# A spectral-mixing and leaky-ReLU kernel: loading filter rows instead of copying them, and a new order of work in the prologue

## Chip, cores and metric

One core of a Trainium2 chip. The metric is the device time of one execution in microseconds (us). In a profile, PE is the matmul engine, DVE is VectorE, ACT is ScalarE, POOL is GpSimd.

## The reference

`x` is (8, 3008, 256), the filters are (1505, 256), `w_in` is (256, 2048), `w_out` is (2048, 256).

```python
X = np.fft.rfft(x, axis=1)
y = np.fft.irfft(X * (filt_r + 1j * filt_i)[None], n=3008, axis=1)   # 24064 tokens
h = y.reshape(24064, 256) @ w_in
out = np.maximum(0.01 * h, h) @ w_out
```

## The kernel before

The transform of a batch is four stages of matmuls with transposes between them: S1, a DVE transpose, S2 (whose result is multiplied by the filters), SA, a second transpose, SB, which writes the tokens into `yts`. The result of each matmul stage is copied out of PSUM, where matmuls write, by ACT or DVE; this is called evacuation. The program uses PSUM in banks and lets a stage write into one only after its last content has been read. From then on the two large matmuls of chunk after chunk of 512 tokens keep PE busy, and the transforms of later batches run beside them. Only the first batch's transform, the prologue, has nothing to hide behind. It is split into two halves of the channels (`hf`). DVE and Pool share the multiplication of S2's result; the filter tiles need the same rows twice, in partitions 0 to 63 and in 64 to 127.

```python
    def filt_load(dst, src, d0, dn):
        for q, first, sgn in ((0, 0, 1), (Q, N1, -1)):
            nc.gpsimd.dma_start(dst[q : q + Q, :, ds(d0, dn)], ...)   # casts to fp16
    ...
    for n0, nn in first_parts:
        x_load(0, n0, nn)                       # 4 loads
    for hf in range(2):
        filt_load(fa_sb, filt_r, hf * DH, DH)   # 2 loads each: 8 in all
        filt_load(fb_sb, filt_i, hf * DH, DH)
    nc.gpsimd.dma_start(i1_sb[:], i1_d.ap())
    nc.gpsimd.dma_start(w_in_sb[:], ...)
    ...
    def first_s2(hf, c, n, on_pool):
        ps = bank("ph", n, DH)                  # 2 banks in turn
        ...                                     # matmuls
        if on_pool:
            ...                                 # ACT copies PSUM to SBUF, Pool multiplies twice
        else:
            ...                                 # DVE multiplies twice, straight from PSUM

    def upper(hf):                              # rows 0-63 copied to 64-127
        for t, cp in ((fa_sb, act), (fb_sb, dve)):
            cp(t[64:P, :, ts(hf, DH)], t[0:64, :, ts(hf, DH)])

    def keep_warm(n):                           # matmuls on a tile of zeros
        ...
    keep_warm(28)
    ...                                         # S1 in four parts, as the parts of x land
    t1_part(0, 0, True)(), t1_part(0, 1, True)()   # the first transpose
    upper(0)
    first_s2(0, 8, 8, True)
    x_load(1)
    first_s2(0, 0, 8, False)
    t1_part(0, 2, True)()
    keep_warm(3)
    first_s2(0, 20, 4, True)                    # Pool's small block
    keep_warm(4)
    first_s2(0, 16, 4, False)
    t1_part(0, 3, True)()
    upper(1)
    first_sa(0, 0), first_sa(0, 16)
    keep_warm(3)
    first_s2(1, 8, 8, True)
    first_s2(1, 0, 8, False)                    # DVE's second half starts here
    first_sa(0, 8), first_sa(0, 20)
    keep_warm(3)
    ...                                         # w_out load
    first_s2(1, 16, 8, False)                   # DVE's last block
    keep_warm(4)
    first_sa(1, 0)
    ...                                         # other SA, second transposes
    for g in range(8):
        first_sb(g, act, ...)
    for g in range(8, 16):
        first_sb(g, (act, dve)[g % 2], ...)
```

Of the kernel before, what the change touches and what calls it, by code (L numbers as in the profile page):

```python
# [20 lines left out]
Q = 32  # L21
# [44 lines left out]
def kernel(  # L66
# [30 lines left out]
    fa_sb = cpool.tile([P, NC, D], FP16, name="fa_sb")  # L97
    fb_sb = cpool.tile([P, NC, D], FP16, name="fb_sb")
# [18 lines left out]
    def bank(kind, n, w):  # L117
        of = wide if kind == "ph" else single
        t = of[turn[kind] % len(of)]
        turn[kind] += 1  # L120
        return t[:, : n * w].rearrange("p (n w) -> p n w", n=n)
# [5 lines left out]
    DH = D // 2  # L127

    def x_load(b, n0=0, nn=N2, d0=0, dn=D):

        for lo, cnt in ((0, R1),) if b + 1 < B else ((0, 64), (64, N1 - 64)):
            nc.gpsimd.dma_start(  # L132
                x_sb[lo : lo + cnt, ds(n0, nn), ds(d0, dn)],
                bass.AP(tensor=x.tensor, offset=x.offset + (b * N + lo * N2 + n0) * D + d0,
                        ap=[[N2 * D, cnt], [D, nn], [1, dn]]))

    def filt_load(dst, src, d0, dn):

        for q, first, sgn in ((0, 0, 1), (Q, N1, -1)):
            nc.gpsimd.dma_start(  # L140
                dst[q : q + Q, :, ds(d0, dn)],
                bass.AP(tensor=src.tensor, offset=src.offset + first * D + d0,
                        ap=[[N1 * D, N2 // 2], [sgn * NC * D, 2], [sgn * D, NC], [1, dn]]))

# [8 lines left out]
    for hf in range(2):  # L153
        filt_load(fa_sb, filt_r, hf * DH, DH)
        filt_load(fb_sb, filt_i, hf * DH, DH)
    nc.gpsimd.dma_start(i1_sb[:], i1_d.ap())
    nc.gpsimd.dma_start(w_in_sb[:], moe_w_in.rearrange("(dt p) c -> p dt c", p=P))
    idle = cpool.tile([P, CH], FP16, name="idle")
# [20 lines left out]
    def paired(t):  # L179
        return t[:].rearrange("p (e n t) -> p n e t", n=Q, t=2)  # L180
# [7 lines left out]
    def t1_part(b, i, flat=False):  # L188
        def go():
            a = big[(4 * b) % 3][:].bitcast(FP32)[:, ts(i, E4 * Q)].rearrange("p (e n) -> p e n", n=Q)  # L190
            o = big[(4 * b + 1) % 3][:].bitcast(FP32)
            if flat:
                o = o[:, ts(i, E4 * Q)].rearrange("p (e n) -> p e n", n=Q)
            else:
                o = o.rearrange("p (n e) -> p e n", n=Q)[:, ts(i, E4), :]
            nc.vector.transpose(o, a)  # L196
        return go
# [49 lines left out]
    two = ("pf", "ph")  # L247
    act, dve = nc.scalar.copy, nc.vector.tensor_copy
# [9 lines left out]
    def first_s2(hf, c, n, on_pool):  # L258
        ps = bank("ph", n, DH)
        src = paired(big[1])  # L260
        for j in range(0, n, 4):
            nc.tensor.matmul(ps[:, ds(j, 4), :].rearrange("p n (e t) -> p n e t", t=2), fwd2,  # L262
                             src[:, ds(c + j, 4), ts(hf, DH // 2)], start=True, stop=True)
        fs = [f[:, ds(c, n), ts(hf, DH)] for f in (fa_sb, fb_sb)]
        if on_pool:
            y = [outp.tile([P, n, DH], FP16, tag="ost", name=f"fy{i}_h{hf}_c{c}") for i in range(2)]
            xs = [scrp.tile([P, 4, DH], FP32, tag=f"p{j // 4 + 1}", name=f"fx_h{hf}_c{c + j}")
                  for j in range(0, n, 4)]
            for j, xf in enumerate(xs):
                act(xf[:], ps[:, ts(j, 4), :])  # L270
            for i in range(2):
                for j, xf in enumerate(xs):
                    nc.gpsimd.tensor_tensor(y[i][:, ts(j, 4), :], xf[:], fs[i][:, ts(j, 4), :], AL.mult)
        else:
            y = [ypp.tile([P, n, DH], FP16, tag=f"yw{i}", bufs=2, name=f"fy{i}_h{hf}_c{c}")
                 for i in range(2)]
            for i in range(2):
                nc.vector.tensor_tensor(y[i][:], ps, fs[i], AL.mult)
        ys[(hf, c)] = y

    def first_sa(hf, c):
        y = ys.pop((hf, c))
        for j in range(0, y[0].shape[1], 4):
            ps = bank("pf", 4, DH)
            for i, m in enumerate((inv2, inv2x)):
                nc.tensor.matmul(ps, m, y[i][:, ds(j, 4), :], start=(i == 0), stop=(i == 1))  # L286
            act(paired(big[2])[:, ds(c + j, 4), ts(hf, DH // 2)],  # L287
                ps.rearrange("p n (t e) -> p n e t", t=2))


    def first_t2(i):
        a = big[2][:].bitcast(FP32)[:, ts(i, E4 * Q)].rearrange("p (e n r) -> p e n r", n=Q // 2, r=2)
        o = big[0][:].bitcast(FP32).rearrange("p (h n e r) -> p h e n r", h=2, n=Q // 2, r=2)
        nc.vector.transpose(o[:, i // 2, ts(i % 2, E4)], a)  # L294

    def first_sb(g, copy, kind):
        dt, h = g // 8, g % 8
        src = big[0][:].rearrange("p (h n e r t) -> p h n r t e", h=2, n=Q // 2, r=2, t=2)
        ps = bank(kind, 4, N1)
        for j in range(4):  # L300
            n2 = 4 * h + j
            for t in range(2):
                nc.tensor.matmul(ps[64 * t : 64 * t + 64, j, :], src[:, dt, n2 // 2, n2 % 2, t, :],  # L303
                                 i1_sb[:, n2, :], start=True, stop=True)
        yv = yts[0][:, dt, :].rearrange("p (a c) -> p a c", c=N2)
        copy(yv[:, :, ds(4 * h, 4)], ps.rearrange("p c a -> p a c"))

    def upper(hf):
        for t, cp in ((fa_sb, act), (fb_sb, dve)):
            cp(t[64:P, :, ts(hf, DH)], t[0:64, :, ts(hf, DH)])  # L310


    def keep_warm(n):
        for _ in range(n):
            nc.tensor.matmul(po_ps.rearrange("p a d -> p (a d)"), idle[:, 0:P], idle[:],  # L315
                             start=True, stop=True)

    keep_warm(28)
    g = 0
    for n0, nn in first_parts:  # L320
        while nn:
            n = 2 if nn % 4 or n0 >= N2 - 4 else 4
            first_s1(n0, n, two[n // 4], (dve, act)[g % 2])
            n0, nn, g = n0 + n, nn - n, g + 1
        keep_warm(5 if n0 < N2 else 14)
    t1_part(0, 0, True)(), t1_part(0, 1, True)()
    upper(0)
    first_s2(0, 8, 8, True)
    x_load(1)
    first_s2(0, 0, 8, False)  # L330
    t1_part(0, 2, True)()
    keep_warm(3)
    first_s2(0, 20, 4, True)
    keep_warm(4)
    first_s2(0, 16, 4, False)
    t1_part(0, 3, True)()
    upper(1)
    first_sa(0, 0), first_sa(0, 16)
    keep_warm(3)
    first_s2(1, 8, 8, True)  # L340
    first_s2(1, 0, 8, False)
    first_sa(0, 8), first_sa(0, 20)
    keep_warm(3)
    nc.gpsimd.dma_start(w_out_sb[:], moe_w_out.rearrange("(ct p) d -> p ct d", p=P))
    first_s2(1, 16, 8, False)
    keep_warm(4)
    first_sa(1, 0)
    keep_warm(4)
    first_t2(0), first_t2(1)
    first_sa(1, 16), first_sa(1, 8)  # L350
    first_t2(2), first_t2(3)
    keep_warm(3)
    for g in range(8):
        first_sb(g, act, two[(g // 2) % 2])
    for g in range(8, 16):
        first_sb(g, (act, dve)[g % 2], two[(g // 2) % 2])

    nc.gpsimd.tensor_scalar(fb_sb[64:P], fb_sb[64:P], -1.0, None, AL.mult)

# [70 lines left out]
    for slot in range(SL * (NCHUNK + 1)):  # L430
        ci, g = divmod(slot, SL)
# [36 lines left out]
```

## Time and profile before

| what | value | where from |
|---|---|---|
| median time | 784.93 us (3 runs); with three later ones 785.34 us (6 runs, 784.69 to 786.42) | timed runs |
| profiled execution | 784.44 us, span 782.6 us | profile |
| start of the first transpose | 17.03 us | DVE's timeline |
| token tile complete (last SB evacuation) | 42.75 us | DVE's timeline |
| gapless PE work begins | 53.49 us | chain that ended last |

The start of the first transpose is called **T1** here, and the way from it to the complete token tile **C**: 42.75 - 17.03 = 25.72 us. The rest, 784.44 - 42.75 = 741.69 us, is not touched by the change. The three views of this profile that the argument starts from are shown in the prediction; the end of C is the line at 42.20 of its first. Its beginning is this line of DVE's timeline (start, length, what, count):

```profile
17.03 2.37 DVE L196 STREAM_TRANSPOSE big<-big 128x1024 f32<-128x1024 f32 x2 [0.21 <-ACT big L184]
```

This is PE's timeline at the beginning (start, length, what, count):

```profile
1.20 8.34 PE L315 MATMUL po_ps<-idle 128*128 128x512 f16 x28 [1.20 <-DVE one L162]
9.38 0.38 PE L253 MATMUL pf<-x_sb,f_sb 94*128 94x256 f16 x2
```

S1 starts when the 28 warm-up matmuls end.

### The profile page before, as it was taken

To read this page: it belongs to the slowest core of one execution; us is meant where nothing else is said; L and a number is where in the kernel's file an instruction comes from. 1 tells how busy PE (TensorE), PEld (TensorE's weight loads), DVE (VectorE), ACT (ScalarE), POOL (GpSimd) and SP (SyncE) were. 2 spreads that over 40 slices of the span, in tenths; PEclk is the share of its full clock that TensorE was granted. 3 is DMA by queue.
4 is the path that set the end of the run, shared out by engine and by line. 5 is a ranking of instruction groups with operands and counts; after the bars stand their busy time and mean duration, and the time that the engine had idled before them with its cause. 6 is when DMAs were issued, how large, how long until landed. Compare 5 with 4: busy or idle time off the path is not lost.

```text
span 782.6 us, 13696 instructions
## 1 busy us (share of the span) xinstructions
PE 775.5 (99%) x5853; PEld 532.1 (68%) x5853; DVE 366.4 (47%) x458; ACT 556.1 (71%) x790; POOL 148.9 (19%) x122
## 2 busy tenths in 40 slices
PE   9999999999999999999999999999999999999998
PEld 4356677666776677766777667776677666676666
DVE  4868751875237641477306754088432765200000
ACT  4786759776686767777687775967768776666664
POOL 4864300250004300052001510025000340000000
PEclk9999999999999999999999999999999999999999
DMA  9952102301041101510105101140101001101111
GB/s 186 216 83 59 41 28 54 97 28 41 28 103 46 41 28 41 107 42 29 41 28 114 35 29 40 42 106 28 41 28 40 30 28 41 41 28 40 42 41 54
DMA packets 36252, 43.38 MB, mean 55 GB/s; under 512 B 8130, under 2 KB 34370, under 8 KB 35522
## 3 DMA queue, kind: packets, MB, share of 16 engines
q0 software_dynamic: 10000, 16.99, 12.4%
q1 hardware_dynamic: 26192, 25.53, 9.3%
q8 instruction: 45, 0.74, 0.4%
q14 instruction: 15, 0.12, 0.1%
HBM read 34.10 MB, written 24.64 MB: 75 GB/s over the span
## 4 chain that ended last, share of the span: by engine, by line
PE 93%; ACT 2%; DVE 1%; issue 1%; ACTq 0%
PE po_ps L390 41%; PE ph L376 41%; PE pf L173 3%; PE pf L240 2%; PE pf L213 2%; PE pf L228 2%; PE pf L390 1%; ACT big L184 1%; ACT gt_c L381 1%; PE ph L262 0%; PE pf L286 0%; DVE big L294 0%; PE po_ps L315 0%; ACT big L287 0%; PE ph L303 0%
## 5 line engine op out<-in xcount | busy, mean ns | idle before, releaser
L381 ACT ACTIVATE gt_c<-ph 128x1024 f16<-128x1024 f32 x376 | 384.8, 1024 | 194.8 <-PE ph L376 193.2
L376 PE MATMUL ph<-yt,w_in_sb 128*128 128x512 f16 (+7 forms) x1728 | 386.7, 351 | 0.4 <-ACT gt_c L381 0.2
L390 PE MATMUL po_ps<-w_out_sb,gt_c 128*128 128x256 f16 x2944 | 381.5, 272 | 0.5 <-ACT ost_c_t L397 0.5
L390 PEld LDWEIGHTS <-gt_c 128*128 128x128 f16 x3008 | 290.6, 98 | 86.8 <-issue 1.7
L376 PEld LDWEIGHTS <-w_in_sb 128*128 128x128 f16 x1728 | 162.9, 98 | 95.3 <-issue 1.0
L221 POOL TENSOR_TENSOR y_b_g<-p_b_g,p_b_g 128x512 f16<-128x512 f32 x84 | 106.9, 1273 | 225.5 <-DVE p_b_g L219 225.5
L196 DVE STREAM_TRANSPOSE big<-big 128x1024 f32<-128x1024 f32 x32 | 55.9, 1844 | 127.1 <-ACT big L184 127.0
L184 ACT CAST big<-pf 128x512 f16<-128x512 f32 x190 | 109.0, 607 | 1.1 <-PE pf L253 1.1
L243 DVE CAST yt<-pf 128x376 f16<-128x376 f32 x112 | 56.3, 544 | 85.7 <-PE pf L240 85.7
L217 DVE TENSOR_TENSOR p_b_g<-pf,fa_sb 128x512 f32<-128x512 f32 x84 | 58.1, 692 | 38.5 <-PE pf L213 35.9
L397 ACT COPY ost_c_t<-po_ps 128x256 f32<-128x256 f32 x184 | 69.4, 377 | 6.7 <-PE po_ps L390 5.6
L204 DVE STREAM_TRANSPOSE big<-big 128x1024 f32<-128x1024 f32 x28 | 51.1, 1934 | 34.7 <-ACT big L184 34.7
L218 DVE TENSOR_TENSOR p_b_g<-pf,fb_sb 64x512 f32<-64x512 f32 x84 | 58.2, 692 | 1.1
L219 DVE TENSOR_TENSOR p_b_g<-pf,fb_sb 64x512 f32<-64x512 f32 x84 | 57.4, 683 | 1.1
L132 POOL DMA_DIRECT2D x_sb<-in_x_dram x12 | 6.6, 553 | 255.4 <-PE pf L173 254.6
L240 PEld LDWEIGHTS <-big 128*128 128x128 f16 x448 | 25.6, 98 | 13.2
L173 PE MATMUL pf<-x_sb,f_sb 94*128 94x256 f16 x224 | 33.8, 272 | 0.1
L213 PE MATMUL pf<-big,small_sb 128*128 128x512 f16 x84 | 31.8, 379 | 0.0
L228 PE MATMUL pf<-y_b_g,small_sb 128*128 128x512 f16 x84 | 31.8, 379 | 0.0
L240 PE MATMUL pf<-i_sb,big 128*128 128x94 f16 x448 | 28.7, 206 | 0.0
L173 PEld LDWEIGHTS <-f_sb 94*128 94x128 f16 x224 | 21.0, 97 | 9.5 <-issue 1.3
L315 PE MATMUL po_ps<-idle 128*128 128x512 f16 x81 | 21.6, 411 | 1.2 <-DVE one L162 1.2
(46 smaller groups left out, 158.4 us busy)
## 6 DMA issues: line engine op xcount, KB each, us to landing
out_dram<-ost_c_t SPq DMA_DIRECT2D x92, 256.0 KB, 2.1
x_sb<-in_x_dram POOLq DMA_DIRECT2D x6, 1536.0 KB, 11.2
x_sb<-in_x_dram POOLq DMA_DIRECT2D x3, 480.0 KB, 9.3
w_in_sb<-in_moe_w_in_dram POOLq DMA_DIRECT2D x1, 1024.0 KB, 14.1
w_out_sb<-in_moe_w_out_dram POOLq DMA_DIRECT2D x1, 1024.0 KB, 11.0
x_sb<-in_x_dram POOLq DMA_DIRECT2D x1, 1024.0 KB, 8.0
f_sb<-fwd_const SPq DMA_DIRECT2D x4, 192.0 KB, 4.8
fa_sb<-in_filt_r_dram POOLq DMA_DIRECT2D x4, 192.0 KB, 12.1
```

Source lines behind the costliest of these rows:

```text
L173: nc.tensor.matmul(ps[:, j, :], f1_sb[:N1, n2, :], x_sb[:N1, n2, :], start=True, stop=True)
L184: copy(paired(dst)[:, ds(n0, nn), ds(e0, de)], ps.rearrange("p n (e t) -> p n e t", t=2))
L217: nc.vector.tensor_tensor(p1[:], ps, fa, AL.mult)
L218: nc.vector.tensor_tensor(p2[0:64], ps[64:P], fb[64:P], AL.mult)
L219: nc.vector.tensor_tensor(p2[64:P], ps[0:64], fb[0:64], AL.mult)
L221: nc.gpsimd.tensor_tensor(y1[:], p1[:], p2[:], AL.add)
L240: nc.tensor.matmul(ps[:, j, :], src[:, dt, n2, :], i1_sb[:, n2, :], start=True, stop=True)
L243: copy(yv[:, :, ds(4 * h, 4)], ps.rearrange("p c a -> p a c"))
L376: nc.tensor.matmul(ph[:, j, ds(o, ln)], w_in_sb[:, dt, ts(ct, P)], yts[b % 2][:, dt, ds(lo, ln)], start=(dt == 0), stop=(dt == NDT - 1),)
L381: nc.scalar.activation(gts[ci][:, ds(2 * g, 2), :], ph, AF.Lrelu)
L390: nc.tensor.matmul(po, gts[ci][:, ct, ts(tj, P)], w_out_sb[:, ct, :], start=(ct == 0), stop=(ct == NCT - 1))
L397: nc.scalar.copy(ost[:, tj % 2, :], po)
```

## The change

The intent: take the second half's two copies off ACT and DVE by loading the upper rows from memory; give DVE its S2 first; let DVE take group 8 of the last evacuations as well; drop nine warm-up matmuls that are then not needed.

```diff
-    def filt_load(dst, src, d0, dn):
+    def filt_load(dst, src, d0, dn, up=0):
...
+    filt_load(fa_sb, filt_r, DH, DH, 64)
+    filt_load(fb_sb, filt_i, DH, DH, 64)
     nc.gpsimd.dma_start(i1_sb[:], i1_d.ap())
...
     upper(0)
+    first_s2(0, 0, 8, False)
     first_s2(0, 8, 8, True)
     x_load(1)
-    first_s2(0, 0, 8, False)
     t1_part(0, 2, True)()
-    keep_warm(3)
-    first_s2(0, 20, 4, True)
     keep_warm(4)
     first_s2(0, 16, 4, False)
+    first_s2(0, 20, 4, True)
     t1_part(0, 3, True)()
-    upper(1)
     first_sa(0, 0), first_sa(0, 16)
     keep_warm(3)
+    first_s2(1, 0, 8, False)
     first_s2(1, 8, 8, True)
-    first_s2(1, 0, 8, False)
     first_sa(0, 8), first_sa(0, 20)
-    keep_warm(3)
+    keep_warm(2)
...
     first_s2(1, 16, 8, False)
-    keep_warm(4)
     first_sa(1, 0)
...
-    keep_warm(3)
+    keep_warm(2)
...
-        first_sb(g, (act, dve)[g % 2], two[(g // 2) % 2])
+        first_sb(g, act if g in (10, 12, 14) else dve, two[(g // 2) % 2])
```

More of the change, by code (lines that the diff above doesn't have):

```diff
@@ L135, in x_load @@
                         ap=[[N2 * D, cnt], [D, nn], [1, dn]]))
-    def filt_load(dst, src, d0, dn):
+    def filt_load(dst, src, d0, dn, up=0):
         for q, first, sgn in ((0, 0, 1), (Q, N1, -1)):
             nc.gpsimd.dma_start(
-                dst[q : q + Q, :, ds(d0, dn)],
+                dst[up + q : up + q + Q, :, ds(d0, dn)],
                 bass.AP(tensor=src.tensor, offset=src.offset + first * D + d0,
```

## The prediction

> **What bounds the kernel now.** I read the page's busy shares first: PE 775.5 us of a 782.6 us span. The change touches only the prologue, the first 43 us in which the FFT of the first batch is made and no output matmul can run yet. PE's 99% says nothing there, since 81 of its matmuls are warm-up ones on a tile of zeros (21.6 us). So the useful view is the chain that ended last, cut to the first 75 us:
>
> ```profile
> 25.51 0.60 DVE fy_h_c L278
> 26.11 1.16 DVE big L196
> ...
> 35.07 2.18 ACT big L287 x4
> ...
> 37.27 2.38 DVE big L294 x2
> ...
> 42.20 0.56 DVE yt L306
> ...
> 53.49 1.97 PE ph L376 x8
> ```
>
> The reader should see three stretches. Up to about 42.8 us VectorE, ScalarE and short matmuls hand over to each other. From 43.6 to 53.5 us the chain is ScalarE's (each 1.02 us activation plus evacuations of batch 1's first stage). After 53.49 us it is PE without a gap to the end. Hence whatever shortens or lengthens the way to 42.8 us moves the end by the same amount, and nothing else in the change can: at most a few us of 785.
>
> The second view is VectorE's timeline in the prologue:
>
> ```profile
> 19.44 0.95 DVE L310 COPY fb_sb<-fb_sb 64x3072 f16<-64x3072 f16 x1
> 21.43 1.23 DVE L278 TENSOR_TENSOR fy_h_c<-ph,fa_sb 128x1024 f16<-128x1024 f32 x1 [1.04 <-ACT fx_h_c L270]
> ...
> 26.04 1.22 DVE L196 STREAM_TRANSPOSE big<-big 128x1024 f32<-128x1024 f32 x1
> 27.29 2.07 DVE L310 COPY fb_sb<-fb_sb 64x3072 f16<-64x3072 f16 x1
> 29.39 1.22 DVE L278 TENSOR_TENSOR fy_h_c<-ph,fa_sb 128x1024 f16<-128x1024 f32 x1
> 30.53 1.21 DVE L278 TENSOR_TENSOR fy_h_c<-ph,fb_sb 128x1024 f16<-128x1024 f32 x1
> 32.12 1.22 DVE L278 TENSOR_TENSOR fy_h_c<-ph,fa_sb 128x1024 f16<-128x1024 f32 x1 [0.37 <-PE ph L262]
> 33.26 1.21 DVE L278 TENSOR_TENSOR fy_h_c<-ph,fb_sb 128x1024 f16<-128x1024 f32 x1
> ```
>
> Two things are to be seen: an idle 1.04 us before the first product (PE first made the S2 for Pool, then the one for DVE), and a copy of 2.07 us that holds the second half. The third view is Pool's timeline:
>
> ```profile
> 15.76 0.58 POOL L156 DMA_DIRECT2D i_sb<-inv_const  x1
> 16.73 0.72 POOL L157 DMA_DIRECT2D w_in_sb<-in_moe_w_in_dram  x1 [0.40 <-DMA fa_sb<-in_filt_r_dram]
> 21.18 2.27 POOL L273 TENSOR_TENSOR fy_h_c<-fx_h_c,fa_sb 128x512 f16<-128x512 f32 x2 [3.73 <-ACT fx_h_c L270]
> ...
> 25.63 0.60 POOL L132 DMA_DIRECT2D x_sb<-in_x_dram  x1
> 26.25 1.17 POOL L273 TENSOR_TENSOR fy_h_c<-fx_h_c,fa_sb 128x512 f16<-128x512 f32 x1
> 27.37 1.17 POOL L273 TENSOR_TENSOR fy_h_c<-fx_h_c,fb_sb 128x512 f16<-128x512 f32 x1
> 29.12 2.38 POOL L273 TENSOR_TENSOR fy_h_c<-fx_h_c,fa_sb 128x512 f16<-128x512 f32 x2 [0.59 <-ACT fx_h_c L270]
> ```
>
> Pool issues loads and multiplies in one queue. Its issues wait: the eight completion semaphores of its loads are used in turn, so each issue waits until the load eight before it has landed (the 0.40 us above). Pool's slack before its first product is 3.73 us.
>
> **What the Trainium skill says.** "DMA: Bandwidth & Descriptors", section Specifications, gives 512 B as the least transfer for line rate. The trace agrees: the filter loads write 256 B packets, and between 15 and 20 us, when little else moves, the queues carry 182 GB/s, against 276 GB/s in 20 to 25 us with the longer rows. The same page, section "Anatomy of one DMA", puts about 2 us of fixed cost on a load, mostly the receipt after the last byte; here the w_out load stops moving at about 42.5 us and is counted as landed at 33.67 + 11.0 = 44.7 us. "SBUF — State Buffer", section "Who interferes with whom", says a VectorE copy in a two-port mode and GpSimd lock each other out. That fits: the same copy took 0.95 us with Pool idle and 2.07 us with Pool multiplying. "TensorE: Matmul & The Clock Gate", section "What's actually happening", says an idle window of about 3.4 us halves PE's clock; the trace shows 1.00 throughout, so it does not say how near that is.
>
> **The change part by part.**
> *Upper rows loaded.* Two copies go: 2.75 us of ScalarE (23.06 to 25.81, off the path: its next work was not waited for) and 2.07 us of VectorE. Four loads of 192 KB come: 786 KB at 180 GB/s is 4.4 us of transfer time. They stand behind the eight filter loads and ahead of inv_const, w_in, batch 1's x and w_out. Landing times from the issues: the last four filter loads of before at 8.68+12.7=21.4, 11.48+10.5=22.0, 13.80+9.4=23.2, 15.06+9.2=24.3 us, so about 1.1 to 1.3 us apiece; the new ones should land at about 25.5, 26.7, 28.0 and 29.2. Everything behind shifts by about 4.3 us: inv_const 25.9 to 30.2 (wanted at 36.9), w_in 30.8 to 35.1 (wanted at 42.3), x of batch 1 38.0 to 42.3 (wanted at 43.45), w_out 44.7 to 49 (wanted at 55.3). All still hidden, x by only 1.1 us.
> *The wait that this adds to Pool.* inv_const and w_in now stand eight places behind the loads that land at 21.4 and 22.0. Their issues therefore end at about 22.0 + 0.3 + 0.7 = 23.0 us, and Pool multiplies only after that: 23.0 in place of 21.18, late by 1.8.
> *S2 for DVE first.* VectorE's first product starts at 20.5 in place of 21.43 (PE's first two matmuls are done then, and the copy ends at 20.39): 0.9 us early, and its last transpose of stage 1 ends at 26.3 in place of 27.26. With the copy gone too, the second half's first product can start at 27.4 (after 1.0 us of matmul) in place of 29.39: 2.0 us won. Its second product waits for the last new load, about 29.3, and ends at about 30.5 (before: 31.74). Pool's S2 comes 0.9 us later, at 22.0, hidden behind the 23.0 above.
> *Where VectorE's gain goes.* PE is in order: S2 for the last block stands behind the inverse matmuls of Pool's small block. Pool: 23.0 + four products (4.45) + x issue (0.6) + two products (2.3) = 30.4 us, against 28.54 before. Then two matmuls (0.43) and two warm-up ones (0.43): that S2 starts at 31.3, against 30.98 before. From there before took 6.27 us to the last evacuation at 37.25 (products 32.12 to 34.47, inverse matmuls, four evacuations); so 37.5 now, 0.3 late. Pool's last block ends at 30.4 + 4.55 = 34.95, just when PE reaches it.
> *The last evacuations.* DVE takes group 8 as well: five of 0.55 us after the last transpose instead of four. Before, group 11 on PE waited for a bank from ScalarE and group 15 for one from DVE; the last DVE evacuation ended 3.1 us after the transposes. Now five in a row from 0.5 us give 0.5 + 5 x 0.53, about 3.2. ScalarE ends about 0.4 us earlier, which nothing waits for. Sum: 0.
> *Nine warm-up matmuls less*: no time of their own, they fill gaps.
> Sum: +0.3 + 0.1 = about +0.4 us.
>
> **The rivals.** (1) *The gain comes through*: if the filter loads land earlier than before or Pool's issues do not block it, Pool starts at 22.1, its small block ends at 29.5, and VectorE's own bank decides: S2 at about 30.2 to 30.5, so 0.5 to 0.8 us won, at best 1.2 (second product right after the first, no load waited for). For it: the change was evidently tuned for it, VectorE's chain is the one shown, and PE's clock was never low. Against it: the 0.40 us wait shows that the issues do block. It gives 783.7 to 784.5. (2) *A load becomes the bound*: the last upper rows land after 30.2, or x after 43.5. For it: all queues are saturated until 42 us, and x has 1.1 us of slack. Against it: order of issue is order of landing here. It gives 785.5 to 786.5. (3) *PE goes cold* in the gaps of about 1.5 us before Pool's and VectorE's results: matmuls at half speed for a few us, +1 to +2. Against it: the gaps are short and warm-up matmuls remain.
>
> **Range and chances.** Weights of 0.5 on +0.4, 0.35 on about -0.9, 0.15 on about +1.2 give +0.1 on 784.93: 785.0 us. The range, 783.7 to 786.2, holds the best and the middling bad case and the 1 us spread of the runs before. 2% is 15.7 us, over a third of the whole prologue, which no part can give or cost: faster 0.01, within 2% 0.98, slower 0.01.
>
> **What would show it.** Right: Pool's first product near 23.0 with a wait on a filter load ahead of the w_in issue; VectorE's second half starting near 27.4; a gap of about 1.5 us on VectorE before its last block, and PE's S2 of that block near 31.3, released through Pool; last evacuation into the token tile ending near 43.1 to 43.2; x landed at 42.3 and not waited for. Wrong: the token tile complete before 42.3 (rival 1); a wait of VectorE or Pool on the filter loads of over 1 us or of PE on x (rival 2); a granted clock under 1.00 before 60 us (rival 3).

## The result

The changed kernel took 784.80 us in the median (6 runs, 784.22 to 785.10), the kernel before 785.34 us (6 runs). The ratio is 0.9991, with a 95% interval of 0.9978 to 1.0004. The difference of 0.5 us is not told apart from zero by these runs. All runs of the two kernels before the last four experiments together do so: 21 of the kernel before have a mean of 785.23 us and 11 of the changed one 784.63, so 0.60 us less, with a 95% interval of about 0.2 to 1.0 (the runs are not all of the same rounds).

The profiles say more. In PE's timeline of the changed kernel, the start differs, although the code up to there is the same:

```profile
1.20 7.87 PE L318 MATMUL po_ps<-idle 128*128 128x512 f16 x28 [1.20 <-DVE one L165]
9.71 0.38 PE L256 MATMUL pf<-x_sb,f_sb 94*128 94x256 f16 x2 [0.65 <-DMA x_sb<-in_x_dram]
...
13.01 0.38 PE L256 MATMUL pf<-x_sb,f_sb 94*128 94x256 f16 x2 [0.96 <-DMA x_sb<-in_x_dram]
```

The warm-up was shorter, but x landed later, and PE waited for it twice (0.65 and 0.96 us). This execution started its first transpose 1.47 us later than the profiled one of before. DVE's timeline after, for the lines of before in the prediction:

```profile
18.50 2.37 DVE L199 STREAM_TRANSPOSE big<-big 128x1024 f32<-128x1024 f32 x2 [0.22 <-ACT big L187]
...
22.04 1.22 DVE L281 TENSOR_TENSOR fy_h_c<-ph,fa_sb 128x1024 f16<-128x1024 f32 x1 [0.18 <-issue]
...
28.97 1.22 DVE L281 TENSOR_TENSOR fy_h_c<-ph,fa_sb 128x1024 f16<-128x1024 f32 x1 [1.11 <-PE ph L265]
30.11 1.21 DVE L281 TENSOR_TENSOR fy_h_c<-ph,fb_sb 128x1024 f16<-128x1024 f32 x1
32.63 1.22 DVE L281 TENSOR_TENSOR fy_h_c<-ph,fa_sb 128x1024 f16<-128x1024 f32 x1 [1.31 <-PE ph L265]
```

The times read best from the first transpose. DVE's second half starts at 28.97 - 18.50 = +10.47 us instead of 29.39 - 17.03 = +12.36, so 1.9 us earlier. Its last block starts at +14.13 instead of +15.09: half of the gain is lost in a wait for PE, which has grown from 0.37 to 1.31 us. The other half stays. The second product at 30.11 follows the first with no wait for the new loads. Pool's timeline after:

```profile
22.43 0.72 POOL L160 DMA_DIRECT2D w_in_sb<-in_moe_w_in_dram  x1 [0.45 <-DMA fa_sb<-in_filt_r_dram]
23.51 2.27 POOL L276 TENSOR_TENSOR fy_h_c<-fx_h_c,fa_sb 128x512 f16<-128x512 f32 x2 [0.36 <-ACT fx_h_c L273]
...
27.97 0.60 POOL L132 DMA_DIRECT2D x_sb<-in_x_dram  x1
28.59 1.17 POOL L276 TENSOR_TENSOR fy_h_c<-fx_h_c,fa_sb 128x512 f16<-128x512 f32 x1
29.72 1.16 POOL L276 TENSOR_TENSOR fy_h_c<-fx_h_c,fb_sb 128x512 f16<-128x512 f32 x1
```

The issue of w_in did wait for a filter load and ended at 23.15 us, as predicted, but Pool then waited another 0.36 us for ACT. From here the chain that ended last runs on, through Pool (start, length, what):

```profile
1.94 11.02 DMA x_sb<-in_x_dram
...
18.50 2.38 DVE big L199 x2
20.92 1.90 PE ph L265 x4
22.84 0.59 ACT fx_h_c L273
...
24.63 1.96 POOL fy_h_c L276 x2
...
28.59 2.29 POOL fy_h_c L276 x2
31.74 0.87 PE ph L265 x2
...
42.60 0.56 DVE yt L309
...
53.87 1.97 PE ph L376 x8
```

It now reaches back to a load of x; the one of before, as the profile gives it, began at 25.51 us on DVE. Then come S2, ACT, Pool's blocks and only after them DVE. The token tile is complete at 43.15 us, so C = 43.15 - 18.50 = 24.65 us, 1.07 less than before, while the rest is 785.03 - 43.15 = 741.88 us.

So there are two questions: does C account for the change, and why do the times not show the full 1.07 us?

### The profile page after: what moved, and what is told of

It is laid out like the page before. It is cut to its first block, busy times and chain, and to the rows that moved or that the text cites. A ratio compares the mean times of both kernels' runs of the same rounds, so it can differ in the third digit from the quotient of the medians. Undisturbed runs are those within 1.5% of the kernel's fastest.

```text
span 783.3 us, 13680 instructions
## 1 busy us (share of the span) xinstructions
PE 773.6 (99%) x5844; PEld 531.3 (68%) x5844; DVE 364.6 (47%) x458; ACT 553.2 (71%) x788; POOL 151.7 (19%) x126
## 3 DMA queue, kind: packets, MB, share of 16 engines
HBM read 35.67 MB, written 24.64 MB: 77 GB/s over the span
## 4 chain that ended last, share of the span: by engine, by line
PE 93%; ACT 2%; DMA 1%; issue 1%; POOL 1%; DVE 1%; ACTq 0%; POOLq 0%
PE po_ps L390 41%; PE ph L376 41%; PE pf L176 3%; PE pf L243 2%; PE pf L216 2%; PE pf L231 2%; DMA x_sb<-in_x_dram 1%; ACT big L187 1%; PE pf L390 1%; POOL fy_h_c L276 1%; ACT gt_c L381 1%; PE ph L265 0%; PE po_ps L318 0%; DVE big L297 0%; DVE big L199 0%
## 5 line engine op out<-in xcount | busy, mean ns | idle before, releaser
L318 PE MATMUL po_ps<-idle 128*128 128x512 f16 x72 | 18.9, 406 | 1.2 <-DVE one L165 1.2
```

## The experiments

Read from the trace of each: T1 and C as above, "Pool" is the start of its first product from T1, and "rest" is the time of the profiled execution less the moment at which the token tile is complete.

| kernel | T1 | Pool | DVE half 2 | DVE last block | C | rest | median us (runs) | ratio to before |
|---|---|---|---|---|---|---|---|---|
| before | 17.03 | +4.15 | +12.36 | +15.09 | 25.72 | 741.69 | 785.34 (6) | |
| before_again | 17.63 | +4.15 | +12.36 | +15.08 | 25.71 | 741.90 | 785.10 (5) | 0.9998 (0.9984 to 1.0012) |
| changed | 18.50 | +5.01 | +10.47 | +14.13 | 24.65 | 741.88 | 784.80 (6) | 0.9991 (0.9978 to 1.0004) |
| after_again | 17.33 | +5.21 | +10.47 | +14.32 | 24.85 | 741.87 | 784.84 (5) | 0.9991 (0.9979 to 1.0004) |
| loads_only | 17.63 | +5.65 | +12.20 | +15.06 | 25.70 | 742.10 | 785.43 (5) | 1.0002 (0.9990 to 1.0015) |
| order_only | 16.41 | +5.00 | +10.53 | +14.52 | 25.04 | 741.65 | 783.84 (5) | 0.9981 (0.9968 to 0.9993) |
| pinned_before | 33.38 | +4.15 | +12.37 | +15.08 | 25.70 | 741.78 | 799.85 (6) | 1.0186 |
| pinned_after | 32.86 | +5.01 | +10.47 | +14.13 | 24.64 | 741.71 | 799.29 (4) | 1.0177 |
| pinned_order_only | 32.95 | +5.02 | +10.53 | +14.53 | 25.06 | 741.70 | 799.89 (4) | 1.0185 |
| pinned_old_split | 33.10 | +5.01 | +10.48 | +14.14 | 24.66 | 741.65 | 799.23 (5) | 1.0176 |
| early_after | 17.89 | +5.02 | +10.48 | +14.14 | 24.65 | 741.88 | 784.39 (5) | 0.9991 (0.9977 to 1.0004) |
| order_late | 17.81 | +5.01 | +10.53 | +13.99 | 24.52 | 741.66 | 783.99 (5) | 0.9987 (0.9975 to 1.0000) |
| early_order_late | 17.05 | +5.01 | +10.53 | +14.00 | 24.53 | 741.69 | 783.38 (5) | 0.9982 (0.9969 to 0.9994) |
| sa_late | 17.23 | +5.02 | +10.48 | +13.95 | 24.46 | 741.86 | 784.14 (5) | 0.9989 (0.9976 to 1.0001) |

All experiments gave correct results. The kernel before had a median of 785.32 us (784.39 to 786.21) in 9 runs beside the first four, 785.21 beside the pinned four (the same 9 runs and one more), and 785.05 (783.86 to 786.08) beside the last four, which ran on another chip than the eight before them.

### Both kernels once more

No edit.

> The kernel before once more, to see how much one execution's first loads differ from another's. Theory A (the landing of x is run-to-run jitter, and the kernel before passes it on to its end): the first transpose starts anywhere from 17.0 to 18.6 us, and the token tile is complete 25.7 us after that, whatever the start (42.8 to 44.3 us). Theory B (the later start of 18.50 us in the changed kernel's profile is caused by the change): the first transpose starts at 17.0 us within 0.2. Time ratio to before 1.000 within 0.0007.

> The changed kernel once more. Theory A: the first transpose starts anywhere from 17.0 to 18.6 us; Pool's first product starts at the later of 23.1 us (its w_in issue, held by the landing of filter loads) and first transpose + 5.0 us; the token tile is complete 19.6 us after Pool's first product, so 42.8 us with a start at 17.0 and 43.2 with one at 18.5. Theory B: the first transpose starts at 18.5 within 0.2 again. Time ratio to before 0.9993, -0.5 us, within 0.0006.

The kernel before started its first transpose at 17.63 us this time, with a warm-up that ended at 10.13 us instead of 9.54; C was the same to 0.01 us. The changed kernel started at 17.33, not at 18.5, so Theory B falls. Pool was released at 22.54, just after its w_in issue ended at 22.45: here the issue held it, 0.2 us longer than ACT would have, and C was 0.2 us longer. Theory A had put Pool at the later of 23.1 us and T1 + 5.0. The w_in issue did not end at 23.1: it came earlier with the earlier landing of x and of the filters behind it. In so far Theory A's fixed 23.1 us was a miss.

### The loads alone

```diff
+    filt_load(fa_sb, filt_r, DH, DH, 64)
+    filt_load(fb_sb, filt_i, DH, DH, 64)
...
-    upper(1)
```

> The kernel before with the upper rows loaded and nothing else changed. Theory A (Pool's queue is now held by the filter loads, and VectorE's copy was not what released its next product, since PE ended its S2 for VectorE only 0.1 us before): VectorE's second half starts at most 0.2 us earlier relative to the first transpose, Pool's first product moves from 21.18 to about 23.1 us, so no gain: ratio 1.0000 to 1.0010. Rival C (the copy was the bound and all of the gain is in its removal): the token tile complete 1.5 to 2.0 us earlier relative to the first transpose, ratio 0.9980.

C is 25.70: nothing gained, and Rival C falls. In the old order the copy was not the only thing ahead of DVE's second half. Without it, DVE waits for PE, which makes Pool's S2 first; the second half starts 0.16 us earlier and that is lost again. This is the one profile in which Pool was held clearly. The first line is of DVE's timeline of loads_only, the others are of Pool's:

```profile
29.83 1.22 DVE L281 TENSOR_TENSOR fy_h_c<-ph,fa_sb 128x1024 f16<-128x1024 f32 x1 [1.98 <-PE ph L265]
...
22.46 0.72 POOL L160 DMA_DIRECT2D w_in_sb<-in_moe_w_in_dram  x1 [1.35 <-DMA fa_sb<-in_filt_r_dram]
23.28 2.29 POOL L276 TENSOR_TENSOR fy_h_c<-fx_h_c,fa_sb 128x512 f16<-128x512 f32 x2
```

A wait of 1.35 us for a filter load, and no wait for ACT afterwards: Pool starts at +5.65 instead of +4.15. In that order Pool had slack and it cost nothing.

### The order alone

The changed kernel without the four new loads:

```diff
-    filt_load(fa_sb, filt_r, DH, DH, 64)
-    filt_load(fb_sb, filt_i, DH, DH, 64)
...
     t1_part(0, 3, True)()
+    upper(1)
```

> The change without the new loads: both copies stay. Pool's first product is not held: it starts 5.0 us after the first transpose (PE's order). Theory A: VectorE still loses 2.07 us to the copy (after its last stage-1 transpose at +9.3), so its second half starts at about +11.4 relative to the first transpose, against 12.36 before and 10.47 in the changed kernel; token tile complete 0.7 to 1.0 us earlier than before relative to the first transpose; ratio 0.9988 to 0.9995. Rival C: no gain, ratio 1.0000.

C is 25.04, 0.68 less than before, at the edge of the 0.7 to 1.0 expected. But DVE's second half started at +10.53 and not at +11.4. The copy took 0.95 us here, not 2.07, since it now fell beside a load issue on Pool instead of Pool's products, and DVE waited another 0.18 us for ACT's copy. These are one line of DVE's timeline and one of Pool's, of order_only:

```profile
25.80 0.95 DVE L311 COPY fb_sb<-fb_sb 64x3072 f16<-64x3072 f16 x1
...
25.86 1.01 POOL L132 DMA_DIRECT2D x_sb<-in_x_dram  x1
```

The issue of x's load took 1.01 us instead of 0.60. That load stands in Pool's queue ahead of its small block, so the block ended 0.4 us later (at +12.77 against +12.38 in the changed kernel), and DVE's last block started 0.39 us later (+14.52 against +14.13). This is what the new loads are worth in the new order: not the copy's time on DVE, but Pool's queue kept free of it. The median of 783.84 us, lower than the changed kernel's, is taken up below.

### A fixed start

```diff
-    nc.vector.memset(big[2]..., 0.0)
+    for _ in range(18):
+        nc.vector.memset(big[2]..., 0.0)
+    pin = cpool.tile([P, 64], FP16, name="pin")
+    nc.vector.memset(pin[:], 0.0)
...
-    keep_warm(28)
+    keep_warm(62)
+    keep_warm(1, pin[:])           # moving operand: the tile that DVE wrote last
```

The kernels after and order_only got the same edit; pinned_old_split is the held changed kernel with `(act, dve)[g % 2]` in the last loop.

> The kernel before with its start held to a fixed time: VectorE repeats a memset 17 times more, and the first stage waits for it (about 17.8 us in place of 8.7 to 10.0), so neither the landing of x nor PE's clock phase in its warm-up moves the first transpose. Theory A (time = 741.85 + start of the first transpose + C, where the change alters only C, 25.72 here): first transpose at about 25.5 us in every run, time 793.0 within 1, spread over the runs under 0.5 us where the kernel before has 1.8. Rival (other sources, such as the output loads or the long PE part, make the spread): spread stays at 1 us or more.

> The changed kernel with the same hold. All loads land long before they are wanted, so Pool's issues hold nothing. Theory A: C = 24.65, so 1.05 us less than the held kernel before, spread under 0.5 us. Theory D (the 0.5 us of the timed runs is all that the change gives, and the 1 us seen between the profiles is chance): 0.5 us less or nothing.

> The order without the new loads, with the same hold. Theory A: C = 25.04, so 0.7 us less than the held kernel before and 0.35 more than the held changed kernel (if the copy on VectorE falls beside Pool's load issue as in the profile, 0.95 us long). Theory E (the order alone is the better kernel, as its 783.84 us against 784.84 say): 1.5 us less than the held kernel before.

> The changed kernel with the old split of the last eight evacuations, with the same hold. The prediction gave the split nothing. Theory A: within 0.15 us of the held changed kernel. Rival: the split gives 0.3 to 0.5 us, as ScalarE's four evacuations there take 2.1 us and its first activation then waits.

The hold was mis-sized. Consecutive memsets took 0.91 us each with 0.28 us between them, so the pin came at 22.6 us and not at 17.8. This is PE's timeline of pinned_before:

```profile
22.61 0.21 PE L318 MATMUL po_ps<-pin,idle 128*128 128x64 f16 x1 [5.94 <-DVE pin L168]
...
24.74 2.34 PE L318 MATMUL po_ps<-idle 128*128 128x512 f16 x5
...
29.01 1.25 PE L318 MATMUL po_ps<-idle 128*128 128x512 f16 x5
```

After 5.94 us of idleness five warm-up matmuls took 2.34 us, later 1.25: PE had gone to half speed, and how long it stayed there was different in the four profiles (the second eight matmuls of S1 took 1.88, 1.32, 1.41 and 1.60 us, in the order of the table). So T1 still moved (32.86 to 33.38), the spread of the times stayed at 1.05 to 1.34 us, and as a measurement of times the hold failed: the held order alone has the same median as the held kernel before (799.89 and 799.85 us), and the held changed kernel is 0.56 us under it in the median, 0.88 in the mean. So the times can't decide between Theory A and Theory D (0.5 us is all). For C it served: no load is anywhere near here, and C came out as 25.70, 24.64 and 25.06, the values of the free kernels. That the change shortens C, by 1.06 us here, the order alone by 0.64, is thus repeated in a second setting. Theory E falls: held alike, the order alone has a longer C than the whole change (25.06 against 24.64) and its median (799.89 us) is not below the changed kernel's (799.29). The profiled run of order_only, the fastest of its five (783.10 us), started early, at 16.41 us; its low median is taken up below. The old split gives 24.66: the split is worth 0.02 us, as the prediction said.

### Pool's small block, and an earlier start

In sa_late (from the changed kernel) and order_late (from order_only), PE no longer has to wait for Pool's small block before DVE's last block. The two early kernels are the changed kernel and order_late with the second edit:

```diff
-    first_sa(0, 8), first_sa(0, 20)
+    first_sa(0, 8)
...
     first_s2(1, 16, 8, False)
+    first_sa(0, 20)
```

```diff
-    keep_warm(28)
+    keep_warm(22)
```

> The changed kernel with only that move of the inverse matmuls. VectorE's own bank comes free at +12.82 and PE's S2 stood at +13.07, so VectorE's last block starts 0.2 us earlier, C = 24.45 where Pool starts at +5.0; where Pool is held, C no longer rises with it until Pool's last block is late (Pool end +1.8 us to the last stage-2 evacuation). Time 0.2 us under the changed kernel, not to be told from it. Rival: Pool's small block does not matter, C = 24.65.

> The order without the new loads, and the inverse matmuls of Pool's small block moved behind the S2 of VectorE's last block, which then waits for its own bank alone. Theory A (in the changed order PE's wait for Pool's small block sets VectorE's last block): that block starts at +14.0 instead of +14.52 after the first transpose, C = 24.5 in place of 25.05, Pool's first product at +5.0; time 0.5 us under the order alone at an equal start, about 784.1 at the mean start of 17.7. Rival (the bank is as late as Pool): C stays at 25.0.

> The changed kernel with 22 warm-up matmuls ahead of the first stage in place of 28, so that the first stage starts when x lands and not when the warm-up ends. Theory H (the new loads tie Pool to the clock of the transfers): the first transpose starts 0.4 to 1.3 us earlier than before (16.2 to 17.3 us), but Pool's first product stays at 22.4 to 23.2 us, at the end of the w_in issue, so more than 5.2 us after the transpose; C (first transpose to complete token tile) rises from 24.65 by as much as Pool is late, and the earlier start is given back: time within 0.3 us of the changed kernel. Rival (Pool waits for ScalarE, as in the first profile): Pool at +5.01, C = 24.65, time 0.5 us less.

> The same with 22 warm-up matmuls ahead. No new loads, so Theory H says that the earlier start is kept: Pool at +5.0, C = 24.5, first transpose 16.2 to 17.3, time about 783.3, the best of all. Rival (PE goes cold or x is as late as the warm-up): granted clock under 1 before 20 us, or a first transpose at 17.7 as before, time 784.1.

C fell to 24.46 and 24.52, as expected to 0.02. DVE's last block now waits 1.11 us, for its own bank, in both; on DVE's timeline of order_late:

```profile
31.80 1.23 DVE L279 TENSOR_TENSOR fy_h_c<-ph,fa_sb 128x1024 f16<-128x1024 f32 x1 [1.11 <-PE ph L263]
```

With that the four loads are worth 24.52 - 24.46 = 0.06 us of C: what they saved went through Pool's small block alone.

Theory H was not put to its test in early_after, although its rival's numbers came (Pool at +5.02, C = 24.65). Pool's timeline shows why:

```profile
21.71 0.72 POOL L160 DMA_DIRECT2D w_in_sb<-in_moe_w_in_dram  x1 [0.34 <-DMA fa_sb<-in_filt_r_dram]
22.91 2.27 POOL L276 TENSOR_TENSOR fy_h_c<-fx_h_c,fa_sb 128x512 f16<-128x512 f32 x2 [0.47 <-ACT fx_h_c L273]
```

The warm-up ended at 8.29 us, but x landed late, PE waited 1.05 and 0.74 us for it, and T1 was 17.89 us: the test condition, an early start, did not come about in this execution. The issue ended at 22.43 and Pool was released by ACT at 22.91. In sa_late, with T1 at 17.23, the issue ended at 21.44: there x landed early, and so did the filters behind it.

The version with the lowest median is early_order_late, 783.38 us, 0.9982 of the kernel before (0.9969 to 0.9994); by ratio, order_only with 0.9981 is as good. It was not timed beside the changed kernel; beside early_after in the same rounds it had the lower median (784.39). Its C and T1 came as expected (24.53 and 17.05), but kernels with all 28 warm-up matmuls also started between 16.41 and 18.50 us, and PE waited 0.56 us for x. That the six fewer warm-up matmuls gained anything is not shown.

## Why the prediction was right or wrong

The time fell into the range (784.80 in 783.7 to 786.2), and "within 2%" was right for the reason given: only the prologue is touched. The mechanism was partly wrong, and the predicted sum of +0.4 us has the wrong sign for C, which fell by 1.07 us. The range, 2.5 us wide, held the right account and the wrong one. Two of its figures came out by luck: the w_in issue ended at 23.15 us (23.0) and the token tile was complete at 43.15 us (43.1 to 43.2), because this execution started 1.47 us later than the profiled one of before. Counted from T1 neither holds.

**What held.** The new DVE half started at +10.47 (predicted 27.4 - 17.03 = +10.4). PE's wait for Pool's small block is the new wait, and the chain runs through it; sa_late and order_late shortened C by 0.19 and 0.52 us when it was taken away. The way from Pool's first product to the end of its small block was 7.37 us (predicted 7.4). The evacuations took 3.16 us after the second transposes (predicted 3.2), and pinned_old_split confirms "Sum: 0". The loads alone gain nothing. Landings: inv_const 21.35 + 9.2 = 30.6 (predicted 30.2), w_in 22.43 + 13.0 = 35.4 (35.1), x of batch 1 27.97 + 15.2 = 43.2 (42.3), used at 43.85 with no wait on the chain. The last of the new loads landed at 20.28 + 8.5 = 28.8 us (29.2), and DVE, which was to wait for it, did not come to its product before 30.11.

**The step that failed: "and Pool multiplies only after that: 23.0 in place of 21.18, late by 1.8."** It set two times against each other that belong to one execution only: loads that land at 22.0 us, and a first transpose at 17.03. Both move. In the profile after, the issue ended at 23.15, but the transpose started at 18.50, so ACT had Pool's input later still. In after_again, early_after and sa_late the issue ended at 22.45, 22.43 and 21.44 and Pool started at 22.54, 22.91 and 22.25. So Pool was late by 0.86 us, PE's order, in place of 1.8; the hold added 0.2 us in one of these four. That is Rival 1 of the prediction, to which it had given 0.35.

**A term that was mis-sized.** From the end of Pool's small block to the last stage-2 evacuation the prediction put 0.86 + 6.27 = 7.1 us; the profile has 37.58 - 30.88 = 6.7 us. Of the two inverse matmuls of Pool's small block only the one for the second product has to wait for Pool. And "Nine warm-up matmuls less: no time of their own" was not quite so: before, four of them stood ahead of the last eight inverse matmuls, and PE began these at 34.44 us, just as DVE ended its last block (34.47); after, the first of them ran at 34.16, ahead of DVE's end (34.98), and seven were left. That is about 0.2 us, an estimate from these starts: no run keeps the nine matmuls in the new order, so their share of C is not shown apart from the order's.

The account of the new C, all from the profile after: 5.01 us from the first transpose to Pool's first product, 7.37 to the end of its small block and 6.70 to the last stage-2 evacuation, 19.08 in all, against 37.25 - 17.03 = 20.22 before; with 2.41 (second transposes) and 3.16 (evacuations) that is 24.65. The prediction's terms for the same way were 6.0, 7.4 and 7.1.

**Why the times show 0.5 us and not 1.07.** In the fourteen profiles T1 + C + rest is the time by construction, the rest lies between 741.65 and 742.10, C is set by the kernel to 0.02 us save for the 0.2 us of the hold in after_again, and T1 of kernels with the same 28 warm-up matmuls runs from 16.41 to 18.50 us. T1 depends on two things that the change does not touch in code: the end of the warm-up (8.82 to 10.13 us) and the landing of x. So a single time carries about 1 us of scatter. With the median of 785.34 for before, 741.8 and 25.72, T1 comes out at 17.8; with 784.80 and 24.65 to 24.85, at 18.2 to 18.4. That is an estimate from the medians. Whether this is chance, or the longer program shifts the first loads a little, the two executions of the changed kernel (18.50 and 17.33) cannot say. This stays open, as does the low T1 of order_only. The 0.60 us of all runs (0.2 to 1.0) fits the 0.87 us by which C is shorter in after_again, and just misses 1.07.

The times don't show either that the new loads pay. Three pairs of kernels differ only in whether the upper rows are loaded or copied and were timed beside each other. With the loads, C was shorter by 0.02, 0.19 and 0.06 us, but the mean time was longer in each: loads_only 785.40 us against 785.23 of before, after_again 784.52 against 783.72 of order_only, sa_late 784.04 against 783.94 of order_late. Only in the held pair was it the other way round (799.11 against 799.75). None of these differences is far from the noise. So the 0.39 us of C is shown in the traces and not in the times.

## What to carry to other kernels

In a prologue, compare traces from an event that the change does not touch, not from time zero: the same kernel's start moved by up to 1.2 us, and by 2.1 us between kernels with the same code up to there, while the stretch after that event repeated to 0.02 us where no load held it. A copy that leaves one engine gains only what the next wait allows: the gain went to an in-order queue behind another engine's small block, and moving those two matmuls was worth more of C (0.52 us) than the four loads (0.39 us), and with them moved the loads were worth 0.06. And before a load's landing time is set against a compute time in a forecast, ask whether both hang on the same earlier load.

## What the Trainium skill lacked or had wrong

- "TensorE: Matmul & The Clock Gate", section "What's actually happening": an idle window halves the clock. Agrees: five matmuls took 2.34 us after 5.94 us of idleness and 1.25 us later. PE's gaps in the changed kernel, up to 0.96 us, left it at full speed (eight matmuls of S1 took 1.04 us after that gap and 1.03 later). What the prediction had misread: the granted clock in the profile is no proof at the start. It reads 1.00 for the first 5 us, in which before's nine warm-up matmuls took 3.80 us of busy time; in pinned_before it does fall to 0.50 between 22.6 and 28.0 us. The page says that the cold phase at the start varies from run to run; here it moved the end of the same 28 matmuls between 8.82 and 10.13 us, and so the start of S1 where x was there. That is more than the change gave.
- "SBUF — State Buffer", section "Who interferes with whom": a copy in a two-port mode and GpSimd exclude each other. Agrees in both directions: the copy took 2.07 us beside Pool's products and 0.95 us beside a load issue, where it was the issue that grew, from 0.60 to 1.01 us. The page speaks of the transfer that is held up; that a product behind the issue in the same queue is delayed too (0.4 us here) it doesn't say.
- "DMA: Bandwidth & Descriptors", section Specifications: agrees that short packets are slow (256 B: 180 GB/s through 18 to 26 us of the changed kernel, with the four more loads; 278 GB/s in 25 to 30 us, as the longer rows come). No page gives the scatter of landing times from execution to execution: the second load of x took 8.6 us from issue to landing in sa_late and 11.0 in the changed kernel, with the same code up to there.
